# A grouped-query attention block on one core: V's loads in pairs behind a semaphore of SyncE

## The chip, the core and the metric

The kernel runs on one core of a Trainium2 chip. The metric is device time in microseconds (us) for one launch that computes both problems of the reference. Lower is better. The core has five engines that each follow their own program in order: TensorE (PE; its weight loads are shown as PEld), VectorE (DVE), ScalarE (ACT), GpSimd (POOL) and SyncE (SP). Transfers are issued here from SP and from ACT only, and 16 DMA engines carry them out. The engines meet through semaphores: an instruction raises one, another waits until it has reached a value.

## The reference

Two problems A and B of the same shape are computed and set side by side in the output. All arrays are bfloat16.

```python
B, Sq, D = 16, 80, 576
Hq, Hkv, Sk, Dh = 32, 16, 512, 128
def ref(x, k_cache, v_cache, wq, wo):
    q = (x @ wq).reshape(B, Sq, Hq, Dh).transpose(0, 2, 1, 3)
    k = jnp.repeat(k_cache, 2, axis=1)
    v = jnp.repeat(v_cache, 2, axis=1)
    scores = jnp.einsum("bhqd,bhkd->bhqk", q, k) * (Dh ** -0.5)
    p = _softmax(scores, axis=-1)
    o = jnp.einsum("bhqk,bhkd->bhqd", p, v)
    return o.transpose(0, 2, 1, 3).reshape(B, Sq, Hq * Dh) @ wo
out = concatenate([ref(A_...), ref(B_...)], axis=-1)
```

## The kernel before

**Units.** The work is cut into 128 units U (`NSU`), 64 for each problem. A unit is one batch row with four KV heads, that is eight query heads. One KV head has 2 x 80 = 160 query rows. 128 of them form a main tile, and the 32 left over of the four heads together form a fifth tile, the remainder. So a unit has five tiles of 128 x 512 scores, numbered T = 5 U + k, with k = 0 the remainder. For each tile PE computes the scores (L782 for remainders, L796 for main tiles), DVE takes the negative maximum (L805), ACT the exponential with its row sum (L809), DVE the reciprocal (L815), POOL the normalisation (L818). P is then transposed: by PE (L824) with a copy by DVE (L830, L832), or, for 78 of the 128 remainders (table `RSEL`), by a DMA transpose that SP issues (`rtr`, L836). PE multiplies with V (`pv`, L870) and ACT copies the result (L886). The q projection (L672, copied by L683 on ACT or L684 on DVE) and the output projection (L923) are spread between.

**Transfers.** K of a unit (`ldk`, L746, 512 KB) comes by a DMA transpose that SP issues. V of a unit (`ldv`, L750, 512 KB) comes by a plain DMA that ACT issues, the first four by SP. The pieces of wq (L647, L650) and wo (L712) are plain DMAs of SP, the x of problem B comes in ten DMA transposes of SP (L615), and the output goes out from SP (L957). K has five buffers (`NK`), V four (`NV`), so V of unit U can't be issued before the PV products of unit U-4 are over. The pieces of weights and of x are called W here. Each has a cycle of its own, the number of a unit near which it is issued.

**The planner.** `_Sched` lists every operation with the resources that it reads and writes and simulates the five engines and the DMA queues with fixed durations. It picks operations greedily, and the program of each engine is the order of planned starts. A `grid=(n, g)` says that an operation isn't planned before g us from the time at which the first PV product of unit n is planned (`tv(n)`, smoothed). The grid only sets the order; on the chip an instruction waits for its semaphores alone. Two marks matter here. `ahead` gives priority over others that are ready. `hard`, which only K has from unit 10 on, adds a real wait: for the last PE operation that the plan has finished at K's planned start. So K is issued on the chip when PE reaches that point, and W, which has no such wait, follows as soon as SP is through with what stands ahead of it. `after` says that an operation isn't planned before another one's start.

Before the change, the grids are: K of U at n = U-6, -1.0 us (`KLEAD`, `GK`); V of U at n = U-2, -3.4 us (`VLEAD`, `GV`); the DMA transpose of a remainder at n = U-2, +0.95 us (`RLEAD`, `GR_`); W at its cycle, -3.7 us (`GW`). In class `_Dma` the planner holds a DMA transpose back while a copy runs and a copy back while a transpose runs.

Of the kernel before, what the change touches and what calls it, by code (L numbers as in the profile page):

```python
# [21 lines left out]
PW = 6  # L22
TLAT = 1.4
VLAT = 1.05
VGEN = 2.75
CLAT = 1.3
KLEAD = 6
GK = -1.0
VLEAD = 2
GV = -3.4  # L30
RLEAD = 2
GR_ = 0.95
GW = -3.7
QL0 = 15.0
QL1 = 11.0
KC = 1.85
VK = 8.0
# [4 lines left out]
VC = 1.5  # L42
# [11 lines left out]
VENG = "act"  # L54
VDUR = 0.42
VU0 = 14
KU0 = 10
# [2 lines left out]
WENG = "sp"  # L60
WOENG = "sp"
NVS = 4
QRING = 1.6
WOC = 1.05
XDMA = True
# [356 lines left out]
def bass_concat_heads__gqa_block_cached__gqa_block_cached__near_ridge_kernel(  # L422
# [18 lines left out]
    NSU = 2 * UPR  # L441
# [8 lines left out]
    with ExitStack() as es:  # L450
# [19 lines left out]
        warm = wo_sb[:, 0, 0:512]  # L470
        ones = wo_sb[:, 1, 0:128]

        sem_names = (["e_pe", "e_act", "e_dve", "e_pool", "d_x00", "d_x01", "d_x10", "d_x11", "d_wo0", "d_wo1",
                      "d_wq0", "d_wq1", "d_wqs", "d_wqt"]
                     + ["d_out%d" % i for i in range(NOSB)]
                     + ["d_r%d" % i for i in range(NPT)]
                     + ["d_k%d" % i for i in range(NK)] + ["d_v%d" % i for i in range(NV)])
# [2 lines left out]
        S = _Sched()  # L480

        def R(res, ver):
            return (res, ver)
# [26 lines left out]
        def em_warmend(e):  # L510
# [4 lines left out]
              name="warm", stream="W", dur=NWARM * 0.427, alloc=[vw])  # L515
# [3 lines left out]
        def em_warm2(e, vw=vw2):  # L519
            last = None  # L520
            for _ in range(NWARM2):
# [4 lines left out]
              name="warm2", stream="X", dur=NWARM2 * 0.3, alloc=[vw2])  # L526
        S.add("dve", -LA - 13.1, em_warmend, reads=[R(vw2, 0)], writes=[R(("warm",), 2)], name="warmend",
              stream="warmset")
# [13 lines left out]
        for half in range(NPP):  # L542
            x_ap = probs[0][0]
            for part, (k0, k1) in enumerate(XP):
                def em_ldx(e, x_ap=x_ap, half=half, k0=k0, k1=k1):
# [5 lines left out]
                      writes=[R(("xs", half * NRT + k_), 0) for k_ in range(k0, k1)], dsem="d_x%d%d" % (half, part),  # L551
                      name="ldx%d.%d" % (half, part), stream="x0", dur=0.5, cost=XC * (k1 - k0))
            for blk in range(NRT):
                rb = half * NRT + blk
                vb = S.bank("M0" if half == 0 else "M1")
                x = (XA + 0.5 * blk if blk < 2 else XA + XB + 0.1 * blk) if half == 0 else XH + 0.8 * blk
# [8 lines left out]
                def em_xev(e, half=half, blk=blk, vb=vb):  # L565
# [4 lines left out]
                      stream="X", dur=_mm(5, 128), lat=0.2, alloc=[vb])  # L570
                S.add("dve", x + 0.3, em_xev, reads=[R(vb, 0)], writes=[R(("xT", half, blk), 0)],
                      name="xev%d" % rb, stream="xev", dur=0.45, lat=0.13)
# [24 lines left out]
        cycle = {}  # L597
        n = 3
        while jobs:
            c_ = [j for j in jobs if j[1] <= n]  # L600
            if c_:
                j = min(c_)
# [2 lines left out]
                assert n <= j[0], (n, j)  # L605
            n += 1

        for half in range(NPP):
            x_ap = probs[1][0]
            st0 = UPR + 16 * half - lead[NG // 2 + 2 * half]  # L610
            for ck in range(5):
                def em_ldxt(e, x_ap=x_ap, half=half, ck=ck):
                    src = x_ap.rearrange("b s d -> (b s) d")[half * NROW:(half + 1) * NROW, :]
                    c0 = ck * 128 if ck < 4 else D - 128
                    return e.dma_start_transpose(xT[:, half, ck:ck + 1, :],  # L615
                                                 src[:, c0:c0 + 128].rearrange("n (c d) -> n c d", c=1))

                S.add("sp", 5.0 * cycle[("x", half, ck)] - 4.0, em_ldxt,
                      writes=[R(("xT", half, b_), 1) for b_ in range(NRT)] if ck == 0 else [R(("xT", half, "t", ck), 1)],
                      dsem="d_x%d0" % half, name="ldxt%d.%d" % (half, ck), stream="x", dur=1.3, cost=0.62, kind="T",  # L620
                      grid=(cycle[("x", half, ck)], GW))

        def qpos(goct, bl):
            return (2 * goct + bl // 4) % NQB * 4 + bl % 4
# [2 lines left out]
        for goct in range(NG):  # L627
            prob, q, half = unit(goct)
            wq_ap = probs[prob][3]
            wv = prob * NOCT + q  # L630
            wsl = wv % 2
            u0 = goct * 8
            pieces = () if half else ((0, 512), (512, 1024)) if goct < 2 else ((0, 1024),)
            for pi, (c0, c1) in enumerate(pieces):
                st0 = u0 - lead[goct]
                t_ld = 5.0 * st0 - 20.0 if goct > 1 else (-90.0, WQ1)[goct] + (10.0, WQ1B)[goct] * pi
                dsem = "d_wqs" if goct == 0 and pi == 0 else "d_wqt" if goct == 1 and pi == 0 else "d_wq%d" % wsl
                eng = ("act", "sp")[goct] if goct < 2 else WENG
                strm = "wqa" if goct == 0 else "wqs" if goct == 1 else "wq"
                if goct < 2:  # L640
                    parts = ((0, 4, c0, c1), (4, 5, c0, c1))
                else:
                    parts = tuple((0, 4, 256 * j, 256 * j + 256) for j in range(4)) + ((4, 5, 0, 1024),)
                for j, (k0, k1, n0, n1) in enumerate(parts):
                    def em_ldw(e, wq_ap=wq_ap, q=q, wsl=wsl, n0=n0, n1=n1, k0=k0, k1=k1):
                        if k0 == 4:
                            return e.dma_start(wq_sb[64:128, wsl, 4, n0:n1],  # L647
                                               wq_ap[512:576, q * 1024 + n0:q * 1024 + n1])
                        src = wq_ap[k0 * 128:k1 * 128, q * 1024 + n0:q * 1024 + n1]
                        return e.dma_start(wq_sb[:, wsl, k0:k1, n0:n1], src.rearrange("(c p) n -> p c n", p=128))  # L650

                    S.add(eng, t_ld + 0.01 * k0 if goct < 2 else 5.0 * cycle[("wq", goct, j)] - 4.0, em_ldw,
                          writes=[R(("wq", wsl, k0 // 4, p_), wv) for p_ in range(n0 // 256, n1 // 256)], dsem=dsem,
                          name="ldw%d.%d.%d.%d" % (goct, pi, k0, n0), stream=strm if goct < 2 or k0 == 0 else "wqb", dur=0.5,
                          cost=(0.12 + 0.8 * WQC if k0 < 4 else 0.4) * (n1 - n0) / 1024.0 * (1.0 if goct < 2 or k0 else 1.25),
                          grid=(cycle[("wq", goct, j)], GW) if goct > 1 else None)

            for i in range(8):
                for c in range(2):
                    if goct == 0:  # L660
                        b0, nb = ((0, 2), (2, 6))[c]
                        x = -LA - ((6.0, 3.6), (1.2, 0.5))[i // 4][c] + (0.6 if i < 4 else 0.05 if c == 0 else 1.2) * (i % 4)
                    else:
                        b0, nb = QB[c]
                        x = 5.0 * (u0 - lead[goct] + i + c * max(QSH, lead[goct] - QS0)) + 1.6
# [34 lines left out]
        for sg in range(2 * NPAIR):  # L700
            prob, hh = divmod(sg, NPAIR)
            wo_ap = probs[prob][4]
            hc = HH // NWC
            base = prob * UPR + hh * NPP * 16
            for n in range(2 * NWC):
                i_, wc = divmod(n, NWC)
                c3 = (sg + i_) % 2
                h0 = hh * HH + wc * hc

                def em_ldwo(e, wo_ap=wo_ap, h0=h0, hc=hc, wc=wc, c3=c3):  # L710
                    src = wo_ap[h0 * 128:(h0 + hc) * 128, c3 * DC:(c3 + 1) * DC]
                    return e.dma_start(wo_sb[:, wc * hc:(wc + 1) * hc, c3 * DC:(c3 + 1) * DC],  # L712
                                       src.rearrange("(h p) n -> p h n", p=128))

                o0_, os_ = OPX[sg] if sg < 3 else (LP0, LPS)
                S.add(WOENG, 5.0 * cycle[("wo", sg, n)] - 4.0, em_ldwo,
                      writes=[R(("wo", c3, wc), sg)]
                      + ([R(("warm",), 3 + c3), R(("ones",), 1 + c3)] if sg == 0 and wc == 0 else []),
                      dsem="d_wo%d" % c3, name="ldwo%d.%d.%d" % (sg, c3, wc), stream="wo", dur=0.5, cost=WOC,
                      grid=(cycle[("wo", sg, n)], GW))  # L720

        qk_order = []
        gsize, gfirst = {}, {}
# [13 lines left out]
        for U in range(NSU):  # L737
            goct, bl = divmod(U, 8)
# [9 lines left out]
            def em_ldv(e, vc_ap=vc_ap, b=b, q=q, vs=vs):  # L748
                src = vc_ap[b:b + 1, 4 * q:4 * q + 4, :, :].rearrange("b g (p j) d -> p b g (j d)", j=4)
                return e.dma_start(v_sb[:, vs:vs + 1, :, :], src)  # L750

            S.add("sp", 5.0 * gfirst[U] + 0.5 * (U - gfirst[U]) - LA - KK, em_ldk, writes=[R(("kT", ks), U)],
                  dsem="d_k%d" % ks, name="ldk%d" % U, stream="K", dur=1.94, cost=KC, kind="T", ahead=100.0 if U >= KU0 else 0.0,
                  grid=(U - KLEAD, GK) if U >= KU0 else None, hard=U >= KU0)
            if True:
                S.add(VENG if U >= NVS else "sp", 5.0 * U - VK, em_ldv, writes=[R(("V", vs), U)],
                      dsem="d_v%d" % vs, name="ldv%d" % U, stream="V" if U >= NVS else "V0", dur=VDUR, cost=VC,
                      ahead=100.0 if U >= VU0 else 0.0, grid=(U - VLEAD, GV) if U >= VU0 else None,
                      kind="V" if U >= NVS else "C")

            vo = None
            rdma = any(a_ <= U < b_ and U % 4 in m_ for a_, b_, m_ in RSEL)
            for k in range(5):
# [87 lines left out]
                if k == 0 and rdma:  # L851
                    S.add("sp", max(tg + RDK, 5.0 * (U - NPT) + 7.0), em_rtr, reads=[R(("P", psl), ("n", T))], writes=pt_writes, dsem="d_r%d" % pts,
                          name="rtr%d" % T, stream="RT", dur=RDD, cost=RDC, ahead=RDO, kind="T",
                          grid=(U - RLEAD, GR_))
                else:
                    S.add("pe", t0, em_tr, reads=[R(("P", psl), ("n", T)), IDENT], writes=[R(vt, 0)],
                          name="tr%d" % T, stream="T", dur=_mm(4, 128), lat=0.2, alloc=[vt])
                    S.add("dve", t0 + 0.44, em_ptev, reads=[R(vt, 0)], writes=pt_writes,
                          name="ptev%d" % T, stream="ptev", dur=0.33, lat=0.13, ahead=PTO)
# [177 lines left out]
```

## Time and profile before

| | |
|---|---|
| median of 3 runs | 778.71 us (775.06 to 784.32) |
| the profiled execution | 772.67 us, of which the span is 770.9 us |
| PE busy | 762.3 us (99% of the span) |
| DVE, ACT, POOL busy | 680.0, 607.2, 432.3 us |
| V's issues on ACT's queue | 124, of 375 ns each (median) |
| K's issues on SP's queue | 128, median 2.7 us, 1.30 to 7.33 us |
| issue to landing, median | K 5.7 us, V 5.0 us, remainders 5.3 us |
| granted TensorE clock | 1.00 |

The span runs from the first to the last instruction of the profiled execution, and 1.8 us lie around it. Busy is the time in which an engine has at least one instruction in work. Waiting instructions, and those that issue DMAs, aren't busy; the latter stand in rows of the queues (SPq, ACTq), where the duration is the time for which the issuing instruction is held. The chain is the work that set the end, followed back from the last instruction.

### The profile page before, as it was taken

The numbers are of one execution on the slowest core, as the hardware profiler recorded it, in microseconds if no ns is written. First come the engines' busy times: TensorE is split into PE (matmuls) and PEld (weight loads), VectorE is DVE, ScalarE is ACT, GpSimd is POOL, SyncE is SP. The second block draws the span as 40 slices with busy tenths as digits, with TensorE's granted clock in tenths as the row PEclk, the third lists the DMA queues.
The fourth block names the chain that finished last, engine by engine and source line by source line (L and its number), as shares of the span: only waits on it lengthen the run. The fifth ranks groups of instructions, "written<-read, shape, count | busy, mean of one in ns | idle before, by whom it ended". The sixth has DMA issues, their size and how long they took to land.

```text
span 770.9 us, 21081 instructions
## 1 busy us (share of the span) xinstructions
PE 762.3 (99%) x7942; PEld 575.7 (75%) x7942; DVE 680.0 (88%) x1599; ACT 607.2 (79%) x1695; POOL 432.3 (56%) x647
## 2 busy tenths in 40 slices
PE   9899999999999999999999999999999999999998
PEld 5577777777777777777777777777777777777786
DVE  4999999899899999999989989988888988899972
ACT  1888987888888888877778877878888888888860
POOL 1556655655656565655555645654656655565650
PEclk9999999999999999999999999999999999999999
DMA  9999999999999999999999999999999999999931
GB/s 245 235 235 244 217 262 217 228 213 228 206 208 226 248 258 255 239 233 228 205 219 202 220 258 238 249 238 241 220 194 207 198 207 240 241 243 241 248 96 31
DMA packets 422660, 170.76 MB, mean 222 GB/s; under 512 B 319264, under 2 KB 422176, under 8 KB 422560
## 3 DMA queue, kind: packets, MB, share of 16 engines
q1 hardware_dynamic: 355872, 103.22, 74.4%
q10 hardware_dynamic: 66688, 66.20, 29.9%
q8 instruction: 64, 1.05, 0.6%
q14 instruction: 36, 0.29, 0.1%
HBM read 87.46 MB, written 2.95 MB: 117 GB/s over the span
## 4 chain that ended last, share of the span: by engine, by line
PE 94%; DVE 4%; DMA 1%; ACT 1%; issue 0%; SPq 0%
PE ps L672 22%; PE ps L923 20%; PE ps L870 18%; PE ps L824 16%; PE ps L796 13%; PE ps L782 4%; DVE negmax L805 2%; DVE pT L832 1%; DMA acc<-in_A_x_dram 1%; ACT p_sb L809 0%; DVE qT L684 0%; DVE xT L566 0%; DVE pT L830 0%; ACT oT L886 0%; PE ps L562 0%
## 5 line engine op out<-in xcount | busy, mean ns | idle before, releaser
L818 POOL TENSOR_SCALAR p_sb<-p_sb,rinv 128x512 bf16<-128x512 bf16 x640 | 429.9, 692 | 315.6 <-DVE rinv L815 315.4
L809 ACT ACTIVATE p_sb<-ps,negmax 128x512 bf16<-128x512 f32 x640 | 438.8, 691 | 63.8 <-DVE negmax L805 53.9
L805 DVE TENSOR_REDUCE negmax<-ps 128x1 f32<-128x512 f32 x640 | 427.5, 682 | 17.8 <-PE ps L782 9.6
L832 DVE COPY pT<-ps 128x512 bf16<-128x512 bf16 x512 | 210.2, 417 | 15.8 <-PE ps L824 13.3
L870 PE MATMUL ps<-pT,v_sb 128*128 128x160 bf16 x2048 | 219.1, 233 | 0.3 <-issue 0.2
L824 PE MATMUL ps<-ident,p_sb 128*128 128x128 bf16 x2248 | 214.6, 219 | 0.3 <-DVE pT L832 0.2
L672 PE MATMUL ps<-xT,wq_sb 128*128 128x320 bf16 (+2 forms) x1280 | 212.6, 299 | 0.8 <-ACT p_sb L809 0.6
L870 PEld LDWEIGHTS ps<-pT,v_sb 128*128 128x128 bf16 x2048 | 163.3, 98 | 42.5 <-issue 2.0
L796 PE MATMUL ps<-kT,qT 128*128 128x512 bf16 x512 | 193.0, 379 | 1.0 <-ACT p_sb L809 1.0
L824 PEld LDWEIGHTS ps<-ident,p_sb 128*128 128x128 bf16 x2248 | 159.8, 98 | 37.4 <-DVE pT L832 5.9
L923 PE MATMUL ps<-wo_sb,oT 128*128 128x288 bf16 x1280 | 171.3, 286 | 0.1
L672 PEld LDWEIGHTS ps<-xT,wq_sb 128*128 128x128 bf16 x1280 | 116.7, 98 | 54.0 <-ACT oT L886 3.8
L923 PEld LDWEIGHTS ps<-wo_sb,oT 128*128 128x128 bf16 x1280 | 122.7, 98 | 34.2 <-issue 2.1
L886 ACT CAST oT<-ps 128x320 bf16<-128x320 f32 x256 | 108.6, 424 | 44.7 <-PE ps L870 42.0
L809 ACT ACTIVATION_READ_ACCUMULATOR p_sb<-ps,negmax 128x1 f32 x640 | 130.3, 204 | 0.0
L684 DVE TENSOR_SCALAR qT<-ps 128x320 bf16<-128x320 f32 (+2 forms) x138 | 67.4, 488 | 13.4 <-PE ps L672 12.1
L683 ACT ACTIVATE qT<-ps 128x320 bf16<-128x320 f32 (+1 forms) x118 | 51.1, 433 | 31.4 <-PE ps L672 30.9
L796 PEld LDWEIGHTS ps<-kT,qT 128*128 128x128 bf16 x512 | 50.0, 98 | 5.6 <-ACT p_sb L809 2.4
L951 DVE TENSOR_TENSOR osb<-ps,acc 128x288 bf16<-128x288 f32 x40 | 18.3, 457 | 26.9 <-PE ps L923 26.5
L782 PE MATMUL ps<-kT,qT 128*32 128x512 bf16 x512 | 39.6, 384 | 1.9 <-ACT p_sb L809 1.9
L815 DVE RECIPROCAL rinv<-rowsum 128x1 f32<-128x1 f32 (+2 forms) x206 | 34.3, 168 | 6.0 <-ACT p_sb L809 5.7
L830 DVE COPY pT<-ps 128x512 bf16<-128x512 bf16 x50 | 20.8, 416 | 2.3 <-PE ps L824 2.0
(19 smaller groups left out, 47.0 us busy)
## 6 DMA issues: line engine op xcount, KB each, us to landing
v_sb<-in_B_v_cache_dram ACTq DMA_DIRECT2D x64, 512.0 KB, 4.8
v_sb<-in_A_v_cache_dram ACTq DMA_DIRECT2D x60, 512.0 KB, 5.1
wo_sb<-in_A_wo_dram SPq DMA_DIRECT2D x16, 288.0 KB, 5.5
wo_sb<-in_B_wo_dram SPq DMA_DIRECT2D x16, 288.0 KB, 5.0
wq_sb<-in_B_wq_dram SPq DMA_DIRECT2D x16, 256.0 KB, 4.8
out_dram<-osb SPq DMA_DIRECT2D x40, 72.0 KB, 3.3
v_sb<-in_A_v_cache_dram SPq DMA_DIRECT2D x4, 512.0 KB, 5.0
wq_sb<-in_A_wq_dram SPq DMA_DIRECT2D x8, 256.0 KB, 5.1
```

Of the source, the lines that this page charges most:

```text
L672: last = e.matmul(ps[:, vb.phys, 0:n1 - n0], lhsT=wq_sb[:, wsl, ck, i * 128:(i + 1) * 128], rhs=xT[:, half, ck, n0:n1], start=(ck == 0), s ...
L684: return e.tensor_scalar(dst, src, SCALE, None, op0=AluOpType.mult)
L782: last = e.matmul(ps[32 * g4:32 * g4 + 32, vb_.phys, :], lhsT=qT[:, qp_, g4 * 160 + 128:g4 * 160 + 160], rhs=kT[:, ks_, :, g4 * 128:(g4 + ...
L796: return e.matmul(ps[:, vb.phys, :], lhsT=qT[:, qp, gl * 160:gl * 160 + 128], rhs=kT[:, ks, :, gl * 128:(gl + 1) * 128], start=True, stop= ...
L805: return e.tensor_reduce(negmax[:, si:si + 1], ps[:, vb.phys, :], axis=AX.X, op=AluOpType.max, negate=True)
L809: return e.activation(p_sb[:, psl, :], ps[:, vb.phys, :], AF.Exp, bias=negmax[:, si:si + 1], scale=1.0, accum_out=rowsum[:, ss, k:k + 1])
L818: return e.tensor_scalar(p_sb[:, psl, :], p_sb[:, psl, :], rinv[:, ss, k:k + 1], 1.0, op0=AluOpType.mult, op1=AluOpType.mult)
L824: last = e.transpose(psb[:, vt.phys, j * 128:(j + 1) * 128], p_sb[:, psl, j * 128:(j + 1) * 128], ident[:])
L832: return e.tensor_copy(pT[:, pts, :, 0:4, gl * 32:gl * 32 + 32], psb[:, vt.phys, 0:512].rearrange("p (j h c) -> p j h c", j=4, h=4))
L870: last = e.matmul(ps[:, vo.phys, off:off + 160], lhsT=v_sb[:, vs, gl, j * 128:(j + 1) * 128], rhs=pT[:, pts, j, :, gl * 32:gl * 32 + 32], ...
L886: return e.copy(dst, src)
L923: last = e.matmul(ps[:, vb.phys, 0:DC], lhsT=oT[:, hi, rb * 128:(rb + 1) * 128], rhs=wo_sb[:, hi, c3 * DC:(c3 + 1) * DC], start=(hi == 0), ...
```

## The change

V's loads from unit 4 on are put in pairs (`VN` = 2): units U0 and U0+1 with U0 even have the same planned time, at grid n = U0-2, +0.5 us. From U0 = 14 on, both depend on a mark, an empty instruction (`nop`) that SP carries out and that raises a new semaphore `e_sp`. There are 57 marks (U0 = 14, 16, ... 126). A mark is planned after the W piece of cycle U0-2 if there is one, and otherwise after K of unit U0+4, with priority over all else on SP. The offsets of the others move: K from -1.0 to -2.6 us, remainders from +0.95 to +0.05 us (even units) and -0.3 us (odd ones), W from -3.7 to -0.65 us (even cycles) and +1.2 us (odd ones). The planner's figure for the generation of a V load goes from 2.75 to 2.55 us. Each later piece of wq gets a semaphore of its own. Which remainders go by DMA is the same as before.

```diff
-VGEN = 2.75
+VGEN = 2.55
-GK = -1.0
+GK = (-2.6, -2.6)
-GV = -3.4
+GV = 0.5
-GR_ = 0.95
-GW = -3.7
+GR_ = (0.05, -0.3)
+GW = (-0.65, 1.2)
+VN = 2
...
+        wname = {}
...
+                wname[cycle[("x", half, ck)]] = "ldxt%d.%d" % (half, ck)
...
-                      grid=(cycle[("x", half, ck)], GW))
+                      grid=(cycle[("x", half, ck)], GW[cycle[("x", half, ck)] % 2]))
...
+            def em_mark(e):
+                return e.nop(nofuse=True)
+
             S.add("sp", 5.0 * gfirst[U] + 0.5 * (U - gfirst[U]) - LA - KK, em_ldk, writes=[R(("kT", ks), U)],
                   dsem="d_k%d" % ks, name="ldk%d" % U, stream="K", dur=1.94, cost=KC, kind="T", ahead=100.0 if U >= KU0 else 0.0,
-                  grid=(U - KLEAD, GK) if U >= KU0 else None, hard=U >= KU0)
-            if True:
-                S.add(VENG if U >= NVS else "sp", 5.0 * U - VK, em_ldv, writes=[R(("V", vs), U)],
-                      dsem="d_v%d" % vs, name="ldv%d" % U, stream="V" if U >= NVS else "V0", dur=VDUR, cost=VC,
-                      ahead=100.0 if U >= VU0 else 0.0, grid=(U - VLEAD, GV) if U >= VU0 else None,
-                      kind="V" if U >= NVS else "C")
+                  grid=(U - KLEAD, GK[U % 2]) if U >= KU0 else None, hard=U >= KU0)
+            if U < NVS:
+                S.add("sp", 5.0 * U - VK, em_ldv, writes=[R(("V", vs), U)], dsem="d_v%d" % vs, name="ldv%d" % U,
+                      stream="V0", dur=0.55, cost=1.5)
+            else:
+                U0 = U // VN * VN
+                if U0 >= VU0 and U == U0:
+                    S.add("sp", 5.0 * U - VK - 0.5, em_mark, writes=[R(("mk", U), U)], name="mark%d" % U, stream="mark",
+                          dur=0.05, lat=0.1, ahead=300.0, after=wname.get(U - VLEAD, "ldk%d" % min(U - VLEAD + KLEAD, NSU - 1)))
+                S.add(VENG, 5.0 * U0 - VK + 0.01 * (U - U0), em_ldv, reads=[R(("mk", U0), U0)] if U0 >= VU0 else [],
+                      writes=[R(("V", vs), U)], dsem="d_v%d" % vs, name="ldv%d" % U, stream="V", dur=VDUR, cost=VC,
+                      ahead=100.0 if U0 >= VU0 else 0.0, grid=(U0 - VLEAD, GV) if U0 >= VU0 else None, kind="V")
...
-                          grid=(U - RLEAD, GR_))
+                          grid=(U - RLEAD, GR_[U % 2]))
```

More of the change, by code (lines that the diff above doesn't have):

```diff
@@ L471, in bass_concat_heads__gqa_block_cached__gqa_block_cached__near_ridge_kernel @@
         ones = wo_sb[:, 1, 0:128]
-        sem_names = (["e_pe", "e_act", "e_dve", "e_pool", "d_x00", "d_x01", "d_x10", "d_x11", "d_wo0", "d_wo1",
+        sem_names = (["e_pe", "e_sp", "e_act", "e_dve", "e_pool", "d_x00", "d_x01", "d_x10", "d_x11", "d_wo0", "d_wo1",
                       "d_wq0", "d_wq1", "d_wqs", "d_wqt"]
+                     + ["d_wq%d_%d" % (i, j) for i in range(2) for j in range(5)]
                      + ["d_out%d" % i for i in range(NOSB)]
@@ L650, in em_ldw @@
                         return e.dma_start(wq_sb[:, wsl, k0:k1, n0:n1], src.rearrange("(c p) n -> p c n", p=128))
+                    if goct > 1:
+                        wname[cycle[("wq", goct, j)]] = "ldw%d.%d.%d.%d" % (goct, pi, k0, n0)
                     S.add(eng, t_ld + 0.01 * k0 if goct < 2 else 5.0 * cycle[("wq", goct, j)] - 4.0, em_ldw,
-                          writes=[R(("wq", wsl, k0 // 4, p_), wv) for p_ in range(n0 // 256, n1 // 256)], dsem=dsem,
+                          writes=[R(("wq", wsl, k0 // 4, p_), wv) for p_ in range(n0 // 256, n1 // 256)],
+                          dsem=dsem if goct < 2 else "%s_%d" % (dsem, j),
                           name="ldw%d.%d.%d.%d" % (goct, pi, k0, n0), stream=strm if goct < 2 or k0 == 0 else "wqb", dur=0.5,
                           cost=(0.12 + 0.8 * WQC if k0 < 4 else 0.4) * (n1 - n0) / 1024.0 * (1.0 if goct < 2 or k0 else 1.25),
-                          grid=(cycle[("wq", goct, j)], GW) if goct > 1 else None)
+                          grid=(cycle[("wq", goct, j)], GW[cycle[("wq", goct, j)] % 2]) if goct > 1 else None)
             for i in range(8):
@@ L715, in bass_concat_heads__gqa_block_cached__gqa_block_cached__near_ridge_kernel @@
                 o0_, os_ = OPX[sg] if sg < 3 else (LP0, LPS)
+                wname[cycle[("wo", sg, n)]] = "ldwo%d.%d.%d" % (sg, c3, wc)
                 S.add(WOENG, 5.0 * cycle[("wo", sg, n)] - 4.0, em_ldwo,
@@ L719, in bass_concat_heads__gqa_block_cached__gqa_block_cached__near_ridge_kernel @@
                       dsem="d_wo%d" % c3, name="ldwo%d.%d.%d" % (sg, c3, wc), stream="wo", dur=0.5, cost=WOC,
-                      grid=(cycle[("wo", sg, n)], GW))
+                      grid=(cycle[("wo", sg, n)], GW[cycle[("wo", sg, n)] % 2]))
         qk_order = []
```

## The prediction

> **What bounds the kernel.** I read the busy shares and the chain first, then pieces of the chain by stretch, then who waited for a DMA, then SP's queue with the DMA rates below it.
>
> ```profile
> PE 762.3 (99%) x7942; PEld 575.7 (75%) x7942; DVE 680.0 (88%) x1599; ACT 607.2 (79%) x1695; POOL 432.3 (56%) x647
> ...
> PE 94%; DVE 4%; DMA 1%; ACT 1%; issue 0%; SPq 0%
> ```
>
> PE has 99% of the span busy and 94% of the chain. The chain by stretch says where the other 6% lie. From 420 to 480 us it is PE alone; around 140 us it is not:
>
> ```profile
> by line: PE ps L923 23.0%; PE ps L672 23.0%; PE ps L870 18.7%; PE ps L824 16.4%; PE ps L796 14.4%; PE ps L782 4.5%
> ```
>
> ```profile
> by line: DVE negmax L805 48.8%; DVE pT L832 19.8%; PE ps L923 14.0%; DVE qT L684 7.8%; PE ps L782 5.7%; DVE pT L830 3.3%; DVE rinv L815 1.6%; issue 0.7%
> ```
>
> Apart from the first 39 us, DVE and ACT hold the chain from 56.1 to 60.6 us, 139.4 to 147.5, 325.3 to 328.2 and 484.5 to 487.4, and for two pieces of 0.43 us: some 19 us. All else after the start is PE's own work. The first question for a change to transfers is then whether any transfer is waited for. In the rows of the tile pT (what PE waited for before L870) and the total of SP's waits:
>
> ```profile
>   DMA pT<-p_sb: 0.2, 1
> ```
>
> ```profile
> SPq L746 <- PE ps L824: 124.7, 31, 7.2
> SPq L746 <- PE ps L796: 122.9, 32, 5.8
> SPq L746 <- PE ps L870: 91.6, 24, 5.5
> ```
>
> One wait of 0.2 us in all, after the start. K's issues (L746) wait for PE in 123 cases: the transfers are paced by PE, not PE by them. From the landings in the trace, V lands 11.6 us ahead of its first use (median; least 8.1), K 9.0 us (least 2.3 up to unit 126; 0.96 at unit 127), the transposed remainders 5.2 us (least 0.07, 0.09 and 0.41, for units 122, 123 and 120). So the profiled execution has nothing to win from earlier transfers. The three timed runs lie 2.4 to 11.7 us above its 772.67 us, their median 6.0; since the margins at the end are nearly zero, a slower transfer there is paid by PE, and I put the excess down to that, as a guess.
>
> **What pairing does to the DMA engines.** SP's queue around 311 us, and the rates in four stretches there:
>
> ```profile
> 305.76 2.27 SPq L746 DMA_TRANSPOSE kT<-in_A_k_cache_dram  x1
> 308.08 0.58 SPq L650 DMA_DIRECT2D wq_sb<-in_B_wq_dram  x1
> 311.06 3.17 SPq L746 DMA_TRANSPOSE kT<-in_A_k_cache_dram  x1
> ```
>
> ```profile
> 311.00:312.50 1.50, 1.50 (x14) 1.14 (x12) 1.50 (x5) 1.16 (x4) 0.57 (x1) 1.00 1.06 339
> 312.50:314.50 2.00, 2.00 (x25) 1.64 (x24) 2.00 (x6) 1.67 (x5) 0.15 (x1) 1.00 1.08 96
> 314.50:315.75 1.25, 1.25 (x15) 1.06 (x14) 1.24 (x4) 0.93 (x3) 1.25 (x3) 1.00 1.27 288
> 365.00:366.25 1.25, 1.25 (x14) 1.00 (x12) 1.25 (x4) 1.10 (x5) 1.10 (x2) 1.00 0.93 328
> 366.25:368.75 2.50, 2.50 (x28) 1.55 (x27) 2.18 (x6) 0.89 (x3) 1.62 (x3) 1.00 1.03 232
> ```
>
> The last figure is GB/s, the one before it the DMA share. Copies run at 339; K's transpose, issued at 311.06 while they run, gets 96 for two us and then 288. The K issued at 365.18, as a copy is nearly through, gets 232 all along, and SP is held for 1.30 us instead of 3.17. So a K that meets copies costs about 1.5 us of DMA time, and 1 to 2 us of SP's. With V in pairs, one meeting in two units should go.
>
> [...]
>
> **The change, part by part.**
>
> *57 marks on SP.* A `nop` of SP isn't in the trace. Between 0 and the shortest issue there, 0.34 us: 0 to 19 us on SP, which waits for PE for 475 us in rows of L746. On PE: 0 where SP has slack; where it has none it is part of the next term.
>
> *V's 124 issues.* Of 375 ns each, as before. At 302.95 one begins under a running CAST of 0.43 us, and the next ACTIVATE starts at 303.05: hidden. In a pair the second is not under the same instruction: up to 57 x 0.375 = 21 us on ACT, which idles 771 - 607 = 164 us. I take 0 on PE. Two V loads back to back exist at the start (SP, 22.71 us, 1.14 us for both; landings 27.4 and 28.9), so the queue takes them without holding the issuer, and they land in 4.7 and 5.6 us.
>
> *ACT's wait for the mark.* This is the new danger. A waiting V load holds all of ACT's program: exponentials (score banks stay taken) and the copies of L886, whose two banks are shared with both projections. In the plan the pair stands 3.1 us behind K's start (+0.5 against -2.6). On the chip the mark comes at K's start plus K's issue, plus 0.58 us where a W piece lies between (31 of the 57 marks, counted from the cycles), plus the nop. From below: K's issue 1.30 us, so 1.9 us at most, no wait. From above: K's issues as now. For even units from 18 on they take 2.15, 2.73 and 4.13 us (10%, median, 90%). Everything over 3.1 us sums to 15 us of waits without W and 35 us with a W at every mark, so some 25. It gathers where SP is full, so that K starts late too: 245 to 315 us (mostly remainder, K and W in each unit), 499 to 525, and from 690 us. For the 13 even K's there, the K issue's end less the first PV product six units back is over 0.5 us by 27 us in sum; 4.8 us at the worst (K issued at 267.08, held 5.14 us), and 2.5, 4.1 and 3.9 in the last three. The earlier K offset doesn't help a SP that has no free time. ACT idles 21%, so short waits vanish and long ones don't. Since K should now meet fewer copies (its even issue follows a W planned to be over), I take K's issue at some 2.2 us, near the 10% row, and 3 us on PE. Both ends stay for the range: 0 and 27.
>
> *V later.* +0.5 instead of -3.4, so the margin of an even V falls from 11.6 to about 6.5 us (two units of 5.9, less 0.5 and 4.7), and an odd V keeps about 11. None is late unless a mark is late by over 6 us: 0. *K 1.6 us earlier, remainders 0.9 to 1.25 us earlier, W later*: nothing waits for them now, so 0 in the profiled execution, but the near-zero margins at the end grow. I let half of the 6 us of excess go. *More semaphores for wq, and the planner's other order*: the 19 us of DVE and ACT on the chain may grow or shrink with any new order; 0, +-6.
>
> **Sum.** 772.67 + 3 (ACT) = 775.7 us for an execution like the profiled one; plus half the excess, 3: 778.7, so about **779 us**, the median of before. No change that can be told: 1% (7.8 us) is about what a measurement of this kernel can tell.
>
> **Rivals.**
> 1. *The mark is late* (slower). K's issues stay as long as now and SP stays full in the three stretches. 27 us of ACT waits there, two thirds of them on PE because they are long against ACT's slack, 18 us; with the excess of 6: 797; half of it 788. It decides once waits in sum pass about 12 us. For: SP's queue from 690 to 734 us has no gap over 0.4 us. Against: long K issues come with copies, and those move. Chance 0.32, taken at 792.
> 2. *The DMA time counts after all* (faster). The excess goes wholly, and the new order has a third of the DVE stretches less: 772.7 - 6 = 767. For: the margins at the end. Against: PE waits 0.2 us for transfers. Chance 0.17.
> 3. *The semaphore never holds* and pairing is only another order: 776 to 781, in the forecast's class.
>
> **Chances and range.** Within 1%: 0.51 (forecast and third rival, 772 to 786). Slower 0.32, faster 0.17. The range reaches from 767 to 797, by the bounds of ACT's wait and both rivals; the forecast's own is 772 to 786.
>
> **What would show it.** Right: the time between copies and K shorter, so K's issue (L746) median near 2.2 us instead of 2.7; V's rows on ACTq in pairs 0.4 us apart; no idle time of ACT that SP ended beyond a few us; remainders with over 1 us of margin at the end; PE still 99% busy. Wrong: rows of ACT waiting for SP of over 12 us, with PE idle behind ACT (L809, L886) at 245 to 315 and from 690 us; or DVE stretches on the chain that sum to far from 19 us; or K's issues unchanged.

## The result and the profile after

The changed kernel takes 816.95 us (median of 4 runs, 812.11 to 819.64); the kernel before took 779.38 us beside it. The ratio is 1.0473, with a 95% interval from 1.0392 to 1.0554. The forecast of no change failed; the time also lies above the range's upper end of 797 us. The sign is that of the first rival, the mark that comes late, at about twice its price. Times here are medians of all executions, while ratios leave out those over 1.5% above the fastest, which are two of the four in each of the runs at 799.04 and 800.64 us below.

The page of the changed kernel, busy shares and chain:

```profile
PE 772.1 (95%) x7942; PEld 577.5 (71%) x7942; DVE 681.9 (84%) x1596; ACT 602.1 (74%) x1698; POOL 432.6 (53%) x647
...
PE 82%; DVE 6%; ACT 5%; ACTq 3%; SPq 2%; issue 1%; DMA 1%
```

PE's share of the span falls from 99% to 95% and of the chain from 94% to 82%. Two queues now have a part of the chain, where before SPq had 0% and ACTq was not named: ACTq, V's issues on ACT, and SPq, the issues of SP. The number of instructions on PE is the same. The span is 43.4 us longer (814.3 against 770.9): PE stands for 42.2 us instead of 8.6, and is busy for 9.8 us more. Four stretches of 60 us (busy time of PE first after the length; last columns clock, DMA share, GB/s):

```profile
180.00:240.00 60.00, 60.00 (x632) 45.91 (x630) 54.59 (x131) 50.05 (x142) 35.54 (x53) 1.00 1.10 212
240.00:300.00 60.00, 53.58 (x536) 38.99 (x534) 45.68 (x108) 43.16 (x126) 31.02 (x47) 0.97 1.09 209
600.00:660.00 60.00, 60.00 (x625) 45.61 (x623) 52.63 (x126) 49.63 (x139) 34.82 (x52) 1.00 0.92 200
720.00:780.00 60.00, 51.29 (x529) 38.43 (x527) 46.38 (x112) 39.63 (x114) 30.63 (x46) 0.97 1.01 210
```

From 180 to 240 us and from 600 to 660, where SP issues no W piece, PE never stands. In the other two, where SP also issues W and stores, PE stands for 6 and 9 us of 60. The chain at one such place, piece by piece:

```profile
263.35 0.23 PE ps L813
263.58 0.38 SPq L754
263.95 0.04 issue
264.00 0.58 SPq L719
264.58 0.04 issue
264.62 0.02 SPq L761
264.64 0.02 issue
264.66 0.38 ACTq L758
265.04 0.04 issue
265.07 0.53 ACTq L758
265.60 0.04 issue
265.64 0.43 ACT oT L903
266.07 0.05 issue
266.12 0.45 PE ps L887 x4
```

This is the hold in one picture. SP is still held by K's issue (L754), then issues a piece of wo (L719), then the mark (L761). ACT, which has stood at the mark, issues V twice (L758) and only then does the copy (L903) that PE needs for its next bank. On ACT's side of the same place:

```profile
260.92 0.24 ACT L826 ACTIVATION_READ_ACCUMULATOR p_sb<-ps,negmax 128x1 f32 x1
264.66 0.94 ACTq L758 DMA_DIRECT2D v_sb<-in_A_v_cache_dram  x2
265.64 0.43 ACT L903 CAST oT<-ps 128x320 bf16<-128x320 f32 x1 [4.47 <-SPq L761]
```

ACT idles 4.47 us, 3.50 of them ahead of the first issue and 0.97 for the two issues. I added this up for the 57 pairs, from the end of ACT's last instruction to V's first issue and to ACT's next instruction: **40.8 us of waiting at marks** (27 pairs wait over 0.2 us, the longest 4.26) and **80.9 us of idle ACT** in all. For the 124 single loads of the kernel before, the same sums are 0.0 and 7.9 us.

Why is SP held? The rows of K's issue:

```profile
L754 SPq DMA_TRANSPOSE kT<-in_A_k_cache_dram x64: 1303/3288/7387, 3.3 to 368.0; - x64
L754 SPq DMA_TRANSPOSE kT<-in_B_k_cache_dram x64: 1856/2996/7504, 374.4 to 762.2; - x64
```

The medians are 3.3 and 3.0 us (2.7 and 2.7 before). Even units, whose K comes before a pair, have 2.5 us; odd units, whose K comes right after one, 3.9 us.

### The profile page after: what moved, and what is told of

Its sections match the earlier page's. It is cut to its first block, busy times and chain, and to the rows that moved or that the text cites. A ratio compares the mean times of both kernels' runs of the same rounds, so it can differ in the third digit from the quotient of the medians.

```text
span 814.3 us, 21141 instructions
## 1 busy us (share of the span) xinstructions
PE 772.1 (95%) x7942; PEld 577.5 (71%) x7942; DVE 681.9 (84%) x1596; ACT 602.1 (74%) x1698; POOL 432.6 (53%) x647
## 4 chain that ended last, share of the span: by engine, by line
PE 82%; DVE 6%; ACT 5%; ACTq 3%; SPq 2%; issue 1%; DMA 1%
PE ps L679 19%; PE ps L940 18%; PE ps L887 15%; PE ps L841 13%; PE ps L813 11%; PE ps L799 4%; DVE negmax L822 4%; ACT p_sb L826 4%; ACTq L758 3%; DVE pT L849 2%; ACT oT L903 1%; SPq L719 1%; DMA acc<-in_A_x_dram 1%; DVE qT L691 1%; SPq L754 1%
## 5 line engine op out<-in xcount | busy, mean ns | idle before, releaser
L887 PE MATMUL ps<-pT,v_sb 128*128 128x160 bf16 x2048 | 221.8, 234 | 11.2 <-ACT oT L903 7.8
L849 DVE COPY pT<-ps 128x512 bf16<-128x512 bf16 x512 | 208.2, 415 | 26.8 <-PE ps L841 25.1
L841 PEld LDWEIGHTS ps<-ident,p_sb 128*128 128x128 bf16 x2248 | 161.5, 98 | 36.4 <-issue 5.1
L903 ACT CAST oT<-ps 128x320 bf16<-128x320 f32 x256 | 109.2, 427 | 71.4 <-PE ps L887 35.8
L826 ACT ACTIVATION_READ_ACCUMULATOR p_sb<-ps,negmax 128x1 f32 x640 | 132.8, 207 | 0.0
L690 ACT ACTIVATE qT<-ps 128x320 bf16<-128x320 f32 (+1 forms) x121 | 52.8, 436 | 29.0 <-PE ps L679 26.9
L968 DVE TENSOR_TENSOR osb<-ps,acc 128x288 bf16<-128x288 f32 x40 | 18.3, 457 | 28.1 <-PE ps L940 27.8
L952 ACT COPY acc<-ps 128x288 f32<-128x288 f32 x40 | 16.0, 399 | 8.2 <-SPq L761 3.6
```

The source lines that it names most:

```text
L826: return e.activation(p_sb[:, psl, :], ps[:, vb.phys, :], AF.Exp, bias=negmax[:, si:si + 1], scale=1.0, accum_out=rowsum[:, ss, k:k + 1])
L841: last = e.transpose(psb[:, vt.phys, j * 128:(j + 1) * 128], p_sb[:, psl, j * 128:(j + 1) * 128], ident[:])
L849: return e.tensor_copy(pT[:, pts, :, 0:4, gl * 32:gl * 32 + 32], psb[:, vt.phys, 0:512].rearrange("p (j h c) -> p j h c", j=4, h=4))
L887: last = e.matmul(ps[:, vo.phys, off:off + 160], lhsT=v_sb[:, vs, gl, j * 128:(j + 1) * 128], rhs=pT[:, pts, j, :, gl * 32:gl * 32 + 32], ...
L903: return e.copy(dst, src)
```

## The experiments

Two theories ran through them, first under the names M and P and then, with P put right, as H and D. **M or H, the hold**: the mark is late, and ACT stands at V's issue with its other work behind it (4.47 us idle above). **P**: the pair costs by itself, which I first put down to its two issues on ACT. **D, the burst**: it costs by itself, because a megabyte in one go delays the DMA transposes of K and of the remainders. O is the rival that the new offsets cost. "Gap" below is ACT's idle time around V's loads, counted as for the 80.9 us.

| V | mark | place of V | time, us | ratio to before (95%) |
|---|---|---|---|---|
| singly | no | -3.4 | 771.35 | 0.9971 (0.9949 to 0.9994) |
| singly | no | +0.5 | 771.99 | 0.9968 (0.9934 to 1.0001) |
| in pairs | no | +0.5 | 799.04 | 1.0245 (1.0155 to 1.0335) |
| singly | 114, one per load | +0.5 | 796.40 | 1.0318 (1.0283 to 1.0354) |
| in pairs (the change) | 57 | +0.5 | 816.95 | 1.0473 (1.0392 to 1.0554) |
| singly | 114, a unit earlier | +0.5 | 773.27 | 0.9985 (0.9955 to 1.0015) |

All have the new offsets. The runs of the kernel before that they are set against have medians of 772.3 to 772.9 us, except for the change itself (779.38); set against 772.4, the change would be 5.8% slower instead of 4.7%.

**Taking the mark away, moving it, taking the pair away, pairing alone.** In the first, V's pairs don't read the mark:

```diff
-                S.add(VENG, ..., em_ldv, reads=[R(("mk", U0), U0)] if U0 >= VU0 else [],
+                S.add(VENG, ..., em_ldv, reads=[],
```

> The changed kernel, with V's pairs no longer reading the mark (SP still issues the 57 empty instructions). Theory M, the mark: ACT's 41 us of waiting ahead of the pairs goes, with the idle time that follows it, and the time falls from 817 to 785 or less, within 1% of the kernel before. Theory P, the pair by itself: the two issues of 0.38 and 0.53 us one after the other still hold ACT for some 40 us in sum, and the time stays at 798 or more. Theory O, the offsets and SP's fuller queue (K's issues of odd units at 3.9 us): 808 or more, since nothing of that changes.

Measured: 799.04 us, 1.0245 (1.0155 to 1.0335). ACT's gap falls to 7.4 us; counted up to the first instruction behind both issues it is 19.6 us, against 88.2 in the changed kernel. So the two issues cost ACT little when it isn't held; and yet some 2.5% remain. By the ratios theory M explains about half of the loss, and the mechanism of theory P is wrong. The profiled execution shows what is in its place. SP's queue and ACT's (two views of it), and the rates:

```profile
258.46 5.37 SPq L754 DMA_TRANSPOSE kT<-in_A_k_cache_dram  x1
263.88 0.58 SPq L719 DMA_DIRECT2D wo_sb<-in_A_wo_dram  x1
264.56 1.21 SPq L853 DMA_TRANSPOSE pT<-p_sb  x1
```

```profile
257.97 0.37 ACTq L758 DMA_DIRECT2D v_sb<-in_A_v_cache_dram  x1
...
258.38 0.53 ACTq L758 DMA_DIRECT2D v_sb<-in_A_v_cache_dram  x1
```

```profile
258.50:260.50 2.00, 2.00 (x21) 1.59 (x19) 1.84 (x5) 1.60 (x6) 0.63 (x1) 1.00 0.84 117
260.50:263.50 3.00, 3.00 (x36) 2.12 (x34) 2.11 (x5) 2.38 (x8) 2.07 (x4) 1.00 1.12 328
263.50:265.00 1.50, 1.50 (x24) 1.14 (x17) 1.50 (x5) 0.95 (x4) 0.34 (x1) 1.00 1.28 164
265.00:266.00 1.00, 1.00 (x14) 0.77 (x12) 1.00 (x4) 1.00 (x4) 1.00 (x2) 1.00 1.28 292
```

The pair is issued at 257.97 and 258.38 us; its megabyte moves from 260.5 to 263.5 at 328 GB/s. By the packets in the trace, ACT's queue moves 324 of these and SP's queue 5. K, issued at 258.46, gets through only after it and holds SP for 5.37 us; the remainder's transpose behind it is issued at 264.56. The chain there, with what PE waited for:

```profile
264.56 4.92 DMA pT<-p_sb
269.48 0.14 issue
269.62 0.44 PE ps L887 x4
```

PE waits for the remainder here. Rows of PE that wait for a remainder or for K sum to 8.9 us in this execution, where PE stands for some 20 us more than before; the rest isn't told apart. In this execution 14 of 78 remainders and 4 K tiles land within 0.2 and 0.4 us of their first use, which I count as waited for (in the chain above 0.14 us lie between landing and use; before: 2 and none; changed kernel: 1 and none). So the mark does guard the transposes, and ACT pays for it.

In the second the mark stands behind K and ahead of W:

```diff
-  after=wname.get(U - VLEAD, "ldk%d" % min(U - VLEAD + KLEAD, NSU - 1))
+  after="ldk%d" % min(U - VLEAD + KLEAD, NSU - 1)
```

> The changed kernel, with each mark planned right behind K, ahead of the W piece. Theory M: 31 of the 57 marks come some 0.6 us earlier, but a K issue held for long still delays them; of 41 us of waits some 20 remain, and the time is 800 to 808. If W alone is what makes the mark late: 785 or less. Theory P or O: 812 to 820.

Measured: 805.36 us, 1.0387 (1.0328 to 1.0447). Waits at marks 36.1 us, gap 70.5. M's time came, but not its figure for the waits (20): they fall by 4.7 us only. W ahead of the mark is at most a small part of the lateness; most of it isn't W.

The third undoes the pairs and the mark and keeps the offsets (`VN = 1`, `GV = -3.4`, no mark):

> The kernel before with the new offsets of K, remainders and W (and the planner's new figure), V singly and without a mark as it was. Theory M or P: 772 to 786, no change. Theory O: most of the loss, 800 or more, with K's issues held longer than 2.7 us.

Measured: 771.35 us, 0.9971 (0.9949 to 0.9994). The offsets don't cost; O falls. K's issues do get longer, as O had it (medians 3.5 and 3.3 us), but nothing waits for them: the remainders land with at least 2.6 us to spare. So the longer K issues here are no loss by themselves.

The fourth is the kernel before with pairs alone (old offsets, `VN = 2`, `GV = 0.5`, no mark):

> The kernel before with V in pairs at +0.5 us and no mark, K, remainders and W at their old offsets. Theory M or O: 772 to 788. Theory P: the pair holds ACT for up to 1 us each time, and K meets two copies in a row: 795 or more.

Measured: 800.64 us, 1.0247 (1.0155 to 1.0339). The pair costs with the old offsets as with the new.

**Telling hold from burst.** Next, single loads, each behind its own mark (`VN = 1`, all else as changed):

> The changed kernel with one V at a time (VN = 1), each behind a mark of its own, so 114 marks instead of 57; all offsets as changed. Theory H, the hold: what costs is ACT standing at a mark, and with twice the marks the time is 800 or more. Theory D, the burst: what costs is a megabyte of V in one go, which delays the next K on SP and with it the next mark; single loads take that away, K's issues of odd units fall from 3.9 to about 3.1 us, and the time is 780 to 792.

Measured: 796.40 us, 1.0318 (1.0283 to 1.0354). No K, V or remainder lands late (least margins 5.9, 2.5 and 3.1 us), and still 3.2% are lost. ACT waits 39 us at marks (21.5 us of them at the 57 marks of even units) and has a gap of 68 us. Who waited for the mark:

```profile
  ACT oT L903: 20.3, 12
  ACT p_sb L826: 9.9, 8
  ACT acc L952: 3.0, 1
```

This is the hold without the burst. D's number fails here; the burst is not needed to make marks late. SP's queue shows what is enough:

```profile
252.20 1.27 SPq L853 DMA_TRANSPOSE pT<-p_sb  x1
253.52 2.17 SPq L618 DMA_TRANSPOSE xT<-in_B_x_dram  x1
255.80 3.71 SPq L754 DMA_TRANSPOSE kT<-in_A_k_cache_dram  x1
259.55 0.58 SPq L719 DMA_DIRECT2D wo_sb<-in_A_wo_dram  x1
```

One V is let go at 255.7 us, behind an x transpose that was itself behind a remainder, the next at 260.2, behind K and W.

The pair planned 2 us later (`GV = 2.5`):

> The changed kernel with the pair planned at +2.5 instead of +0.5 us; the mark stands where it stood. Theory H: the wait counts from the pair's place in ACT's program, so of 41 us of waits under 12 remain, and the time is 785 to 798. Theory D: the burst is as large, only later, and meets the odd K more squarely: 805 or more, with K landing later.

Measured: 807.83 us, 1.0454 (1.0405 to 1.0503). Waits fall from 41 to 29 us, not to 12. K's issues of odd units rise from 3.9 to 4.5 us, and PE waits for pT (2% of the chain). The time is D's and not H's, but K doesn't land later (median margin 9.6 us, 9.5 in the changed kernel). That the burst takes what the hold gives back is a reading; the run doesn't tell the two apart.

The pairs issued by SP in its own order, no mark (`VENG = "sp"`, with the planner's figures for a copy of SP):

> The changed kernel with V's pairs issued by SP in its own order, without a mark: ACT issues no transfer from unit 4 on and is never held. Theory H: the whole loss goes, 770 to 785. Theory D: the burst stays, now ahead of K on SP's own queue; K and the remainders land late as in the run without a mark, 790 to 805.

Measured: 796.17 us, 1.0316 (1.0275 to 1.0357), as D said. With ACT out of it, PE waits for transfers; DMA has 6% of the chain. Here V itself is among the late, 11 times:

```profile
PE ps L887 <- DMA v_sb<-in_A_v_cache_dram: 6.0, 3, 2.6
...
PE ps L887 <- DMA v_sb<-in_B_v_cache_dram: 5.3, 3, 2.6
```

The second V of a pair 2 us after the first, both behind the mark:

```diff
-  grid=(U0 - VLEAD, GV) if U0 >= VU0 else None
+  grid=(U0 - VLEAD, GV + 2.0 * (U - U0)) if U0 >= VU0 else None
```

> The changed kernel with the second V of a pair planned 2 us after the first; both behind the same mark. Theory H: the wait for the mark stays (41 us), but the second issue of 0.53 us no longer follows a held one; ACT's gap around V falls from 81 to about 55 us, and the time is 800 to 808. Theory D: the burst is broken in two, 785 to 797, with K's odd issues shorter.

Measured: 797.42 us, 1.0315 (1.0281 to 1.0350). Waits stay at 40 us, the gap falls to 59, about as H said, and the time falls more than H said; but K's odd issues hardly change (4.0 us), and remainders land late again (4% of the chain is DMA). Neither number held.

**The missing corner, the bytes, the hold by itself.** Single loads at the later place, without a mark:

> The new offsets, V singly, no mark, but V planned at +0.5 us as in the changed kernel instead of -3.4: the fourth corner beside the pair without a mark, the single loads with marks and the changed kernel. Theories H and D alike: neither hold nor burst, 768 to 778. If the later place of V costs by itself: 785 or more.

Measured: 771.99 us, 0.9968 (0.9934 to 1.0001). With this the table above is complete: the pair alone costs 2.5%, the mark alone 3.2%, both 4.7%, neither nothing. For the pair the interval is 1.6 to 3.3%, from two executions. This run and the pairs without a mark differ in the pairing alone, apart from 57 empty instructions and the planner's order. K's issues here, and there:

```profile
L754 SPq DMA_TRANSPOSE kT<-in_A_k_cache_dram x64: 1302/2628/8009, 3.3 to 351.9; - x64
L754 SPq DMA_TRANSPOSE kT<-in_B_k_cache_dram x64: 1307/2380/6847, 357.6 to 726.3; - x64
```

```profile
L754 SPq DMA_TRANSPOSE kT<-in_A_k_cache_dram x64: 1302/3559/8183, 3.3 to 358.8; - x64
L754 SPq DMA_TRANSPOSE kT<-in_B_k_cache_dram x64: 1763/3258/9211, 365.2 to 747.2; - x64
```

The pair lengthens them by some 0.9 us (medians), and the longest time from K's issue to its landing goes from 10.7 to 18.3 us.

The pair without a mark, two of four KV heads in each V load:

```diff
+  src = vc_ap[b:b + 1, 4 * q:4 * q + 2, :, :]...
+  return e.dma_start(v_sb[:, vs:vs + 1, 0:2, :], src)
```

> The changed kernel without the mark's read, and from unit 4 on each V load brings two of its four KV heads (half the bytes; the output is therefore not the reference's), so that a pair is 512 KB. Theory D, the burst of bytes: the loss of the pair without a mark (2.5%) goes, 766 to 778, and K and the remainders land with over 2 us to spare. If two issues or the order of the program cost and not the bytes: 788 to 802 as before.

Measured: 770.44 us, 0.9969 (0.9946 to 0.9993). The loss of the pair is gone, with the same two issues in the same place and the same order of instructions on every engine; the remainders have at least 4 us to spare. K's issues:

```profile
L754 SPq DMA_TRANSPOSE kT<-in_A_k_cache_dram x64: 1302/2362/7628, 3.3 to 350.1; - x64
L754 SPq DMA_TRANSPOSE kT<-in_B_k_cache_dram x64: 1302/2003/3827, 356.5 to 718.4; - x64
```

The run also moves fewer bytes in all. That this isn't the reason is the point of the run before it, where all bytes move, one V at a time, and nothing is lost.

One copy on ACT that the plan doesn't know, behind V's load in each even unit:

```diff
+  if U >= VU0 and U % 2 == 0:
+      e.copy(dmy[:] (128x1024), ident broadcast)
```

> The new offsets, V singly at -3.4 us, no mark, and behind V's load in every even unit from 14 on one copy on ACT of 128x1024 into a spare tile, which the plan doesn't know of: some 1.1 us each, 57 times, 60 us in sum. It measures the disputed cost, an unplanned hold of ACT, by itself. Theory H: PE loses about half of it, 790 to 805. If ACT's idle time (22%) takes a hold of 1 us: 770 to 778.

Measured: 783.93 us, 1.0129 (1.0064 to 1.0193). The holds:

```profile
L762 ACT COPY dmy<-ident 128x1024 bf16<-128x1024 bf16 x57 | 59.5, 1043 | 0.2
```

59.5 us on ACT cost 783.93 - 771.35 = 12.6 us, a fifth; neither range had that. Single loads with late marks lose 796.40 - 771.99 = 24.4 us for a gap of 68, over a third. As far as two runs show it, ACT's idle time takes most of short, regular holds and less of irregular ones, where single waits reach 2.6 us.

More remainders by DMA (88) with the new offsets and single loads:

> The new offsets, V singly at -3.4 us, no mark, and 88 instead of 78 remainders transposed by DMA (all of units 62 to 76, every second of 46 to 62). The new offsets alone left the remainders over 2.6 us of margin. If this margin is real room: ten remainders less on PE at 0.22 us each, 2 us, so 767 to 771. If the DMA engines have none: 775 or more, with remainders landing late.

Measured: 783.17 us, 1.0114 (1.0057 to 1.0172). The margin wasn't free room, though not for the reason given: the remainders land in time, and DVE waits for the output's stores instead. They are issued late. For the longest wait, at 403 us, the trace has the store's data ready at 381.07 us and its issue on SP at 400.65, behind the transposes of K, x and the remainders; with the offsets alone no store stands for over 8.4 us. The granted clock (0.991 in the mean) also falls to half for two stretches of 6.83 us, which is some 6 of the 11 us lost (an estimate: half of PE's busy time in them, 5.64 and 6.04 us).

```profile
DVE osb L968 <- DMA out_dram<-osb: 12.3, 3, 6.1
```

**Is it the lateness?** The 114 marks again, each behind K of the unit before:

```diff
+VN = 1
-  after=wname.get(U - VLEAD, "ldk%d" % min(U - VLEAD + KLEAD, NSU - 1))
+  after="ldk%d" % min(U - VLEAD + KLEAD - 1, NSU - 1)
```

> As the run with single V loads and 114 marks, but each mark planned behind K of the unit before, some 6 us sooner. Theory H, lateness: no mark is late, ACT has no idle time that SP ended, and the time is that of single loads without marks, 768 to 777. If the 114 waits, empty instructions or semaphore raises cost by themselves: 785 or more.

Measured: 773.27 us, 0.9985 (0.9955 to 1.0015), waits 3.6 us, gap 11.2. The marks, the waits and the semaphore are free; being late is what costs. One thing moves along with the lateness: the planner also puts other instructions elsewhere, some 1550 of PE's 7942 by more than two places against the late marks. That this order costs by itself isn't excluded by this run; against it stand the 39 us that ACT waits at late marks and 3.6 here.

The changed kernel with its marks and half the bytes in each V load (edit as above):

> The changed kernel with its marks; from unit 4 on each V load brings two of its four KV heads (half the bytes, so the output is not the reference's). If the marks are late mainly because the burst lengthens K's issues: the 41 us of ACT's waits fall below 12, and the time is 770 to 780. If they are late for what stands on SP anyway (W, remainders, K's own issue): 15 to 30 us of waits remain and the time is 782 to 795.

Measured: 775.98 us, 1.0029 (1.0005 to 1.0053), waits 6.4 us, gap 28.9. PE, DVE, POOL and SP have the same instructions in the same order as in the changed kernel, so the order isn't what costs there. With half the bytes most of the marks are in time. How much of this is the burst and how much the smaller load on the DMA engines isn't told apart: single loads of full size with 57 marks weren't tried. In the run with 114 marks those of the even units alone hold ACT for 21.5 us, so about half of the 40.8 us may need no burst.

The offsets alone once more:

> The new offsets of K, remainders and W alone, V singly and without a mark, again with more rounds: 0.994 to 1.000 of the kernel before. Theory: nothing waits for transfers in most executions of the kernel before, so there is little to win beyond its slower executions.

Measured: 771.34 us, 0.9984 (0.9956 to 1.0011). Of the two comparisons one is just clear of 1 and one isn't: no difference that I would claim.

## Why the prediction was wrong

*What bounds the kernel.* Right: PE does, and nothing waited for transfers. So the change could only lose.

*What pairing does to the DMA engines.* This is the step that failed first. I read 96 GB/s behind copies as a price for each meeting of K and copies, and counted meetings: half as many. (SP's queue, and so K, had 77 of the 96; the slip doesn't matter.) But the price isn't fixed. The K issued at 258.46 us behind a pair without a mark's read stood behind its megabyte, 3 us (260.5 to 263.5), and then paid a slow start as well (164 GB/s from 263.5 to 265.0). With single loads in the same place K's issues are 2.6 and 2.4 us, with pairs 3.6 and 3.3, so half as many meetings cost more in sum. The loss of 2.5% isn't the longer issue itself, which the offsets alone have too. As far as the trace shows it, it is what lands late behind it: 14 remainders and 4 K tiles.

*ACT's wait for the mark.* I put 0 to 27 us, took 3 on PE, and found 40.8 us of waits. My own sign of being wrong came, too: rows of ACT that wait for SP sum to 22.7 us. The term was named with its mechanism; the size was wrong, for two reasons. I took K's issue at 2.2 us because K would meet fewer copies. The even K's, which the mark waits for, came near to that (2.5 us), but the odd ones, right behind a pair, rose from 2.6 to 3.9, and then the even K itself starts late: ahead of 22 of the 27 late pairs SP had been issuing for 8.8 us or more with no pause over 0.2 us. And the three stretches were taken for the only ones. They have 18.5 of the 40.8 us, if each pair is put where the kernel before issues its K; 22.3 stand elsewhere, as from 417 to 493 us of the new trace (five pairs, 10.7 us, one of 4.3).

*V's 124 issues.* Hidden, I said, and this holds where ACT isn't held: the gap of the pairs without a mark is 7.4 us. Behind a late mark no instruction runs that could hide them, and the pair then costs 1.0 us (0.97 at 264.66). Of the 80.9 - 40.8 = 40 us of further gap, 28 are those of the 27 late pairs. I had worked out both terms, each as if the other weren't there.

*57 marks on SP, V later, K and remainders earlier.* Right: a mark takes 17 ns on SP, and 114 marks in time cost nothing; V lands 3.9 us or more ahead, the offsets alone are neutral. *Half of the excess of the timed runs.* The excess was nothing steady: beside the experiments the kernel before itself has medians of 772.3 to 772.9 us. Whether its tight margins make its slower executions (up to 782.1 us) stays open.

*The first rival* had the right sign and chain of causes at 788 to 797 us. What it lacks to 817 I put down to the waits beyond 27 us, the unhidden issues and the half clock below; no run gives each its share.

## What to carry to other kernels

A transfer that an engine issues amid work that others need must never wait on something that can be late (ACT stood 40.8 us at the marks here): price such a wait by all that stands ahead of the semaphore's raiser, and put the raise a unit earlier if you can (with 114 marks that took the waits from 39 to 3.6 us). Price collisions of transfers by their bytes and not by their number: here two loads of 512 KB in one go made the next K wait 3 us for both, and with half the bytes the loss of 2.5% was gone (ratio 0.9969). And when two costs share an instruction, ask whether the one takes away the cover of the other.

## What the runs showed of the hardware

Three long stalls of the changed kernel cost twice. After the stall at 263 us (PE busy 0.58 us of 3.14), the granted clock (third column from the end) falls to half:

```profile
262.98:266.12 3.14, 0.58 (x5) 0.16 (x3) 0.69 (x1) 0.48 (x2) 1.85 (x3) 1.00 0.98 163
267.50:270.40 2.90, 2.90 (x20) 1.23 (x17) 1.33 (x3) 1.86 (x6) 0.00 (x0) 0.50 1.12 280
```

The trace has three such windows, at 267.0, 495.7 and 724.4 us, of 3.41 us each, behind gaps of ACT of 4.5, 5.3 and 3.8 us; at half speed they cost some 5 us in sum (an estimate: half of 3 x 3.41). The profiled execution of the kernel before has none while PE works. In the 3.41 us ahead of the three drops PE was busy for 0.87, 0.44 and 0.68 us, and its longest pauses around them were 2.56, 3.78 and 2.73 us; at 267.0 it had been at work again for 0.87 us. The drops lie 228.69 us apart. What sets their times is not shown.
